# Key and query projections in neighbouring PSUM banks, numerators across two banks, and one VectorE instruction where there were two

## The chip, the core and the metric

The kernel is one program on one core of a Trainium2 chip. The metric is the time of the program on the device, in microseconds (us). The core has five engines that each work through their own queue in order: TensorE (PE, matmuls), VectorE (DVE), ScalarE (ACT), GpSimd (POOL) and SyncE (SP, which issues most DMAs). An engine waits where the next instruction of its queue is not ready. PSUM, where matmuls write, has eight banks of 512 float32 per partition.

## The reference

Random-feature attention, and then a mixture of eight experts of which each token takes the best one:

```
q_s, k_s = q * D**-0.25, k * D**-0.25
phi(x):  proj = x @ omega.T;  h = proj - sum(x*x)/2;  h -= max(h);  exp(h)/sqrt(m)
q_p, k_p = phi(q_s), phi(k_s)
kv = k_p.T @ v;  z = sum over s of k_p
out = (q_p @ kv) / (q_p @ z + 1e-6)                     # 8 batches, 8 heads, 576 x 64, 128 features
x = out, rows of 512 (4608 tokens)
e = argmax(x @ w_gate);  gate = softmax(x @ w_gate)[e];  eom = sigmoid(x @ w_output_gate)
y = gate * eom[e] * (relu(x @ w1[e]) @ w2[e])           # 8 experts, 512 -> 1024 -> 512
```

## The kernel before

**Attention** runs in 32 units `u`: a stage `j` of two batches (four stages) times a head (eight). A unit has 1152 rows in nine chunks of 128. For three groups `g` of three chunks TensorE projects keys and queries (`pp`, line 502): keys on its upper 64 rows, queries on its lower 64, each side into a bank of its own. VectorE then takes, for each side apart, the largest of 128 features of three chunks (`least`, line 524, a minimum, since the sign is turned) and turns it into the bias of the exponential (`bias`: line 530 in the first eight units, which fold the squares into the matmul, lines 533 and 537 in the others). ScalarE makes the exponentials from PSUM (`exps`, line 543, three instructions of 128 features for a side and group) and sets the bank free. The keys' exponentials and the values give `kv` (line 639), which gets eight gate columns twice through lines 677 to 700. The queries' exponentials are turned (by TensorE in the first eight units, later by a DMA transpose, line 620) and multiplied with `kv` (`attend`, line 713): a numerator `pn` of 81 columns for each of nine chunks, chunks 0 to 4 in one bank and 5 to 8 in another. `divide` (lines 722, 724, 726) makes, for each of the two banks, the divisor, its reciprocal, and the product `xf`.

**Routing.** Behind the eighth unit of a stage, `route`, `counts` (`pos`, lines 890 to 900), `ranks`, `places`, `table`, `assign` and `lists`, a chain of some fifty small VectorE instructions, sort the stage's tokens by expert. TensorE makes the list of tokens (`pid`, line 1146), VectorE turns it into indices (`gi`, line 1178; for the last list a small matmul `again`, line 1162, comes between). 38 **items** of up to 128 tokens of one expert follow: GpSimd gathers the rows (`gx`, line 1436), a DMA turns them (`xt`, line 1448), TensorE computes `ph` (line 1473) in two halves of 48 matmuls and `po` (line 1504) in two halves of 12. Lists 0, 1 and 2 hand out 8, 8 and 9 items, and the last list the other 13. An item can start only when its list exists, its rows are gathered, and they are turned.

**What sets the order.** `Plan.order` is a list scheduler in Python. Each step names its engines, costs, predecessors and banks. The planner always emits the step that can start first by its own costs and, among steps within 0.1 us, the one of the lowest rank. Attention's ranks lie below those of the items, so the items fill the holes of attention. The emitted order is each engine's queue, and on the chip an engine never leaves it. Units up to 11 take any of eight banks; later units have five (class `a`), items three (class `b`). A bank is taken when a step starts and set free by the last step that reads it.

Of the kernel before, what the change touches and what calls it, by code (L numbers as in the profile page):

```python
# [10 lines left out]
F32 = mybir.dt.float32  # L11
# [3 lines left out]
AF = mybir.ActivationFunctionType  # L15
ALU = mybir.AluOpType
# [18 lines left out]
W = 1 + D + GW  # L35
FC = F // P
# [87 lines left out]
class Plan:  # L124
# [16 lines left out]
    def add(  # L141
        self, key, engine, cost, fn, after=(), rank=0.0, tiles=(), bank=None, frees=(), dma=0.0, turn=False, early=None, cols=None,
        lead={},
# [7 lines left out]
        s.update(frees=frees, dma=dma, turn=turn, tiles=sorted(set(tiles)), early=early, part=self.part, lead=lead)  # L151
# [29 lines left out]
    def order(self):  # L181
# [17 lines left out]
        bank_cls["e"] = range(b0)  # L199
        dma_free = 0.0  # L200
# [4 lines left out]
        while ready:  # L205
            best = None
            for k in ready:
# [3 lines left out]
                if s["bank"]:  # L211
                    free = sorted(bank_free[b] for b in bank_cls[s["bank"][0][0]] if b in bank_free)
                    t = max(t, free[len(s["bank"]) - 1] if len(free) >= len(s["bank"]) else 1e9)
# [11 lines left out]
            for cls, name, _ in s["bank"]:  # L225
                b = min((b for b in bank_cls[cls] if b in bank_free), key=lambda b: bank_free[b])
                del bank_free[b]
                self.bank_of[name] = b
# [36 lines left out]
def attention_moe(ctx: ExitStack, tc: tile.TileContext, kqt, kqn, v, om, wg, w1, w2, cf, cm, ci, out):  # L265
# [38 lines left out]

    plan = Plan({"a": 5, "b": 3})
# [15 lines left out]


# [82 lines left out]
    nb = buf("nb", 2, [NC], F32)  # L405
# [47 lines left out]
    def unit(u):  # L453
# [52 lines left out]
        for g in range(G):  # L506
            x = min(g, len(parts) - 1)
            before_ = [("lo", u, x), ("const", "omh")]
            if g or u:
# [4 lines left out]
                bank=[(cls, ("pp", 2 * u + i, g), [4, M]) for i in range(2)], cols=3072.0 if whole else 1152.0,  # L514
# [3 lines left out]
        for i, nm in enumerate(("k", "q")):  # L518
            n = 2 * u + i

            def least(g, n=n):

                pp = banks["pp", n, g]
                nc.vector.tensor_reduce(out=pp[:, 3, 0:3], in_=pp[:, 0:3, :], op=ALU.min, axis=AX.X)  # L524

            def bias(g, i=i, n=n):
                c = slice(3 * g, 3 * g + 3)
                pp = banks["pp", n, g]
                if whole:
                    nc.vector.tensor_scalar(nb(n)[:, c], pp[:, 3, 0:3], SK, LIFT, ALU.mult, ALU.add)  # L530
                    return
                sq = sqs(u)[:, i, c]
                nc.vector.scalar_tensor_tensor(
                    out=pp[:, 3, 4:7], in0=pp[:, 3, 0:3], scalar=SK, in1=sq, op0=ALU.mult, op1=ALU.add
                )
                yield
                nc.vector.scalar_tensor_tensor(  # L537
                    out=nb(n)[:, c], in0=pp[:, 3, 4:7], scalar=LIFT, in1=sq, op0=ALU.add, op1=ALU.subtract
                )

            def exps(g, n=n):
                for c in range(3 * g, 3 * g + 3):
                    nc.scalar.activation(  # L543
                        ef(n)[:, c, :], banks["pp", n, g][:, c % 3, :], AF.Exp, bias=nb(n)[:, c : c + 1], scale=-SK
                    )

            for g in range(G):
                plan.add(
                    ("mx", n, g), ("DVE",), 0.47, lambda g=g, f=least: f(g), after=[("pp", u, g)], rank=R + i,
                )  # L550
                plan.chain(
                    ("nb", n, g), ("DVE",), (0.1,) if whole else (0.1, 0.1), lambda g=g, f=bias: f(g), rank=R + i,
                    after=[("mx", n, g)] + ([] if whole else [("sqr", u)]), tiles=[("nb", n)] + ([] if whole else [("sqs", u)]),
                )
                plan.add(
                    ("ex", n, g), ("ACT",), 0.76, lambda g=g, f=exps: f(g), after=[("nb", n, g)], rank=R + i,
                    tiles=[("nb", n), ("ef", n)], frees=[("pp", n, g)],
                )
# [1090 lines left out]
```

## Time and profile before

| what | value |
|---|---|
| median of three runs | 665.9 us (665.75, 665.9 and 674.13) |
| the profiled execution | 672.7 us, of which its span is 670.9 us |
| mean granted TensorE clock in it | 0.956 |
| PE busy | 614.1 us, 92% of the span |
| DVE busy | 423.9 us, 63% |
| ACT busy | 413.4 us, 62% |
| POOL busy | 341.3 us, 51% |

"Busy" of an engine is the union of its instructions' recorded times. An instruction on VectorE can be recorded from before the one ahead of it has ended, so the sum of the recorded times is above the busy time. A wait is put down to what ended it. The granted clock (PEclk) is the share of full speed at which TensorE was let run in a stretch.

### The profile page before, as it was taken

The numbers are of one execution on the slowest core, as the hardware profiler recorded it, in microseconds if no ns is written. First come the engines' busy times: TensorE is split into PE (matmuls) and PEld (weight loads), VectorE is DVE, ScalarE is ACT, GpSimd is POOL, SyncE is SP. The second block draws the span as 40 slices with busy tenths as digits, with TensorE's granted clock in tenths as the row PEclk, the third lists the DMA queues.
The fourth block names the chain that finished last, engine by engine and source line by source line (L and its number), as shares of the span: only waits on it lengthen the run. The fifth ranks groups of instructions, "written<-read, shape, count | busy, mean of one in ns | idle before, by whom it ended". The sixth has DMA issues, their size and how long they took to land. (4 is left out here: it accounts for less than half of the span.)

```text
span 670.9 us, 22907 instructions
## 1 busy us (share of the span) xinstructions
PE 614.1 (92%) x8732; PEld 484.2 (72%) x8732; DVE 423.9 (63%) x1271; ACT 413.4 (62%) x970; POOL 341.3 (51%) x235
## 2 busy tenths in 40 slices
PE   6999975889988999999989989999999899999972
PEld 6899864767676777777767777777777677686761
DVE  4899897867749899667876976562783521431160
ACT  5876896679768877888867677863611511431150
POOL 1352455659854887879658668875131122121220
PEclk9999988689988999999997989999999899999996
DMA  9544688898899898889997675666947555732730
GB/s 315 209 130 127 184 282 206 231 210 193 232 364 239 187 239 207 218 220 271 336 212 202 148 162 151 117 138 201 240 102 222 177 86 175 232 85 66 261 110 14
DMA packets 145900, 129.15 MB, mean 192 GB/s; under 512 B 104270, under 2 KB 127440, under 8 KB 144464
## 3 DMA queue, kind: packets, MB, share of 16 engines
q1 hardware_dynamic: 139760, 107.45, 62.3%
q0 software_dynamic: 5984, 19.72, 9.0%
q8 instruction: 86, 1.41, 0.9%
q14 instruction: 70, 0.57, 0.3%
HBM read 83.86 MB, written 19.30 MB: 154 GB/s over the span
## 5 line engine op out<-in xcount | busy, mean ns | idle before, releaser
L1473 PE MATMUL ph<-xt,w1h 128*128 128x128 f16 (+1 forms) x2432 | 209.4, 220 | 2.4 <-ACT hh L1480 0.9
L1473 PE MATMUL ph<-xt,w1l 128*128 128x128 f16 (+1 forms) x1216 | 204.9, 220 | 2.0 <-DVEq L1397 1.0
L543 ACT ACTIVATE ef<-pp,nb 128x128 f32<-128x128 f32 x576 | 164.4, 391 | 46.5 <-DVE nb L537 26.7
L1473 PEld LDWEIGHTS <-w1h 128*128 128x128 f16 x2432 | 184.5, 100 | 11.4 <-issue 1.9
L1484 DVE SCALAR_TENSOR_TENSOR hl<-ph,hh 128x512 f16<-128x512 f32 (+1 forms) x76 | 50.7, 667 | 118.5 <-ACTq L1402 74.4
L566 POOL TENSOR_TENSOR es<-ef,es 128x1152 f16<-128x1152 f32 x44 | 105.2, 2392 | 37.2 <-ACT es L564 29.7
L1473 PEld LDWEIGHTS <-w1l 128*128 128x128 f16 x1216 | 120.0, 100 | 2.5 <-DVEq L1397 1.4
L524 DVE TENSOR_REDUCE pp<-pp 128x3 f32<-128x384 f32 x192 | 103.1, 557 | 23.2 <-PE pp L502 18.2
L1436 POOL DMA_INDIRECT gx<-rows,gi x38 | 39.1, 1030 | 133.1 <-ACT os L1557 100.0
L1504 PE MATMUL po<-w2h,hh 128*128 128x512 f16 x280 | 106.4, 380 | 0.0
L1504 PE MATMUL po<-w2h,hl 128*128 128x512 f16 x280 | 106.1, 379 | 0.0
L1504 PE MATMUL po<-w2l,hh 128*128 128x512 f16 x280 | 106.1, 379 | 0.0
L1504 PEld LDWEIGHTS <-hh 128*128 128x128 f16 x560 | 51.4, 98 | 54.9 <-issue 0.4
L1480 ACT ACTIVATE hh<-ph 128x512 f16<-128x512 f32 (+1 forms) x76 | 44.6, 586 | 75.0 <-PE ph L1473 62.2
L1557 ACT ACTIVATE os<-po,gx 128x512 f32<-128x512 f32 (+1 forms) x38 | 25.5, 670 | 69.5 <-PE po L1504 62.2
L436 POOL TENSOR_TENSOR xlo<-xt,xhi 128x1152 f16<-128x1152 f32 x24 | 57.1, 2381 | 19.8 <-ACT xhi L429 19.4
L564 ACT CAST es<-ef 128x1152 f16<-128x1152 f32 x44 | 50.8, 1165 | 11.0 <-DMA et<-es 8.0
L713 PE MATMUL pn<-kvs,et 128*128 128x81 f16 (+1 forms) x960 | 48.0, 209 | 9.0 <-DMA et<-es 3.2
L713 PEld LDWEIGHTS <-et 128*128 128x128 f16 (+1 forms) x960 | 41.0, 105 | 16.1 <-issue 4.5
L1504 PEld LDWEIGHTS <-hl 128*128 128x128 f16 x280 | 27.4, 98 | 33.1 <-issue 0.2
L747 POOL TENSOR_TENSOR xs<-xf,xs 128x576 f16<-128x576 f32 x32 | 42.0, 1312 | 17.4 <-DVE xs L743 16.3
L502 PE MATMUL pp<-omh,xhi 64*128 64x128 f16 x432 | 43.3, 224 | 4.1 <-ACT ef L543 2.8
(181 smaller groups left out, 1059.8 us busy)
## 6 DMA issues: line engine op xcount, KB each, us to landing
r<-w SPq DMA_DIRECT2D x10, 2048.0 KB, 8.8
xt<-kqt SPq DMA_DIRECT2D x32, 576.0 KB, 5.3
xn<-kqn SPq DMA_DIRECT2D x24, 576.0 KB, 5.5
rawv<-v SPq DMA_DIRECT2D x32, 325.0 KB, 4.2
rows<-xs SPq DMA_DIRECT2D x16, 576.0 KB, 4.9
r<-w SPq DMA_DIRECT2D x8, 512.0 KB, 7.1
ef<-w SPq DMA_DIRECT2D x2, 512.0 KB, 3.9
et<-w SPq DMA_DIRECT2D x2, 512.0 KB
```

The lines of the kernel that those rows point to most:

```text
L436: lambda t0=t0, t1=t1: nc.gpsimd.tensor_tensor(out=xl(u)[:, t0:t1], in0=xt32(u)[:, t0:t1], in1=xh(u)[:, t0:t1], op=ALU.subtract),
L502: nc.tensor.matmul(banks["pp", 2 * u + i, g][:, c, :], x[r, t], w[r, :], start=(a == 0), stop=(a == len(ops) - 1))
L524: nc.vector.tensor_reduce(out=pp[:, 3, 0:3], in_=pp[:, 0:3, :], op=ALU.min, axis=AX.X)
L543: nc.scalar.activation(ef(n)[:, c, :], banks["pp", n, g][:, c % 3, :], AF.Exp, bias=nb(n)[:, c : c + 1], scale=-SK)
L564: nc.scalar.copy(es(slot_es(n))[:, 0], ef(n))
L566: nc.gpsimd.tensor_tensor(out=es(slot_es(n))[:, 1], in0=ef(n), in1=es(slot_es(n))[:, 0], op=ALU.subtract)
L713: nc.tensor.matmul(pn[lo:hi, c - c0, :], a[:, c, lo:hi], w[:, b, :], start=(i == 0), stop=(i == len(ops) - 1))
L747: nc.gpsimd.tensor_tensor(out=x[:, :, P + o : P + o + D], in0=xf(u)[:, :, 0:D], in1=x[:, :, o : o + D], op=ALU.subtract)
L1473: nc.tensor.matmul(ph[:, f4, 0:w_], w[qd][:, kk, fo : fo + P], xt(n)[:, x, 0:w_], start=(a == 0), stop=(a == 3 * KC - 1))
L1480: nc.scalar.activation(hh(n)[:, sl, 0:w_], banks["ph", n, g][:, :, 0:w_], AF.Relu)
L1484: nc.vector.scalar_tensor_tensor(out=hl(n)[:, sl, 0:w_], in0=banks["ph", n, g][:, :, 0:w_], scalar=0.0, in1=hh(n)[:, sl, 0:w_], op0=ALU.ma ...
L1504: nc.tensor.matmul(po, x(n)[:, f, :], w[f // 2][:, f % 2, :], start=(f == 0 and a == 0), stop=(f == FC - 1 and a == 2))
```

## The change

Three things, and what they need in the planner:

- PSUM is one tile of eight banks, and a step's banks are views of it. A step can ask for banks that lie beside each other (`beside`). The planner waits for a pair of free neighbours and, among pairs that are free, takes the one with the fewest free banks next to it.
- Keys' and queries' projections of a group lie in neighbouring banks. `least` and `bias` take both sides in one instruction, 2 x 3 results, and the bias tile `nb` holds both sides of a unit. `exps` stays three instructions for each side and now waits for the bias of both.
- The numerators of all nine chunks lie in two neighbouring banks at a step of 105 columns, so that no chunk crosses from one bank into the next. `attend` writes all nine and `divide` takes all nine at once: three instructions where there were six.

```
-                bank=[(cls, ("pp", 2 * u + i, g), [4, M]) for i in range(2)], ...
+                bank=[(cls, ("pp", 2 * u + i, g), [4, M]) for i in range(2)], beside=True, ...
...
-                pp = banks["pp", n, g]
-                nc.vector.tensor_reduce(out=pp[:, 3, 0:3], in_=pp[:, 0:3, :], op=ALU.min, axis=AX.X)
+            pp = both_sides(g)
+            nc.vector.tensor_reduce(out=pp[:, :, 3, 0:3], in_=pp[:, :, 0:3, :], op=ALU.min, axis=AX.X)
...
+        for g in range(G):
+            plan.add(("mx", u, g), ("DVE",), 0.9, lambda g=g: least(g), after=[("pp", u, g)], rank=R)
+            plan.chain(("nb", u, g), ("DVE",), (0.1,) if whole else (0.1, 0.1), lambda g=g: bias(g), ...)
...
-                    ("mx", n, g), ("DVE",), 0.47, lambda g=g, f=least: f(g), after=[("pp", u, g)], rank=R + i,
...
-                    ("ex", n, g), ("ACT",), 0.76, lambda g=g, f=exps: f(g), after=[("nb", n, g)], rank=R + i,
+                    ("ex", n, g), ("ACT",), 0.76, lambda i=i, g=g: exps(i, g), after=[("nb", u, g)], rank=R + i,
...
-        for c0, c1, pe, dve in ((0, 5, 0.6, 0.48), (5, NC, 0.42, 0.4)):
-                ("pn", u, c0), ("PE",), pe, lambda c0=c0, c1=c1: attend(c0, c1), ..., bank=(cls, ("pn", u, c0), [c1 - c0, W]),
-                ("xf", u, c0), ("DVE",), (0.07, 0.1, dve), lambda c0=c0, c1=c1: divide(c0, c1), ...
+            ("pn", u), ("PE",), 1.02, attend, ..., bank=[(cls, ("pn", u, i), [512]) for i in range(2)], beside=True,
+            ("xf", u), ("DVE",), (0.08, 0.1, 0.85), divide, ...
...
+        def places(s):
+            cls, n = bank_cls[s["bank"][0][0]], len(s["bank"])
+            if s["beside"]:
+                return [tuple(range(b, b + n)) for b in cls if b + n - 1 in cls]
+            return list(itertools.combinations(cls, n))
+        def pick(s, t):
+            ...
+            return min(places(s), key=lambda bs: (late(bs), alone(bs), bs))
...
-                    t = max(t, free[len(s["bank"]) - 1] if len(free) >= len(s["bank"]) else 1e9)
+                    t = max(t, min(max(bank_free.get(b, 1e9) for b in at_) for at_ in places(s)))
...
-                banks[name] = ps.tile([P, *shape], F32, tag=f"bank{b}", name="_".join(str(x) for x in name))
+                banks[name] = shaped(psum[:, plan.bank_of[name], 0 : math.prod(shape)], shape)
```

The other costs, ranks, shifts and the counts of items stay. Since the planner works with other costs and other places for banks, it emits another order on all engines. Three places:

VectorE, groups 1 and 2 of one unit (`pp_1` and `pp_2`; the higher number of a name is the queries' side) before:

```order
L524 TENSOR_REDUCE pp_2_5601<-pp_2_5601 128x3
L533 SCALAR_TENSOR_TENSOR pp_1_5573<-pp_1_5573,sqs_4157 128x3
L533 SCALAR_TENSOR_TENSOR pp_2_5601<-pp_2_5601,sqs_4157 128x3
L537 SCALAR_TENSOR_TENSOR nb_5392<-pp_1_5573,sqs_4157 128x3
L537 SCALAR_TENSOR_TENSOR nb_5392<-pp_2_5601,sqs_4157 128x3
L524 TENSOR_REDUCE pp_1_5574<-pp_1_5574 128x3
```

And VectorE at one group of a unit after the change, where lines 555, 564 and 568 are the old 524, 533 and 537, and `psum` stands for every bank:

```order
L555 TENSOR_REDUCE psum<-psum 128x2x3
L776 CAST xs_6350<-xf_6976 128x9x64
L1409 UNCONDITIONAL_BRANCH
L564 SCALAR_TENSOR_TENSOR psum<-psum,sqs_5520 128x2x3
L568 SCALAR_TENSOR_TENSOR nb_6658<-psum,sqs_5520 128x2x3
L478 TENSOR_REDUCE sqs_7028<-sqt_6654 128x9x2
```

One chain of three per group is left where two ran side by side, and inside it each step reads what the one ahead of it in the chain wrote.

TensorE behind the list of tokens of stage 1 (`pid`) before, the first row of each step (`ph_0_5497` and `ph_1_5626` belong to the eighth item, `ph_0_5994` to the ninth, the first that needs this list):

```order
L1146 MATMUL pid_5399<-r_itc,place 128x16
...
L713 MATMUL pn_0_5428<-kvs_5046,et_5182 128x81
...
L1473 MATMUL ph_0_5497<-xt_4752,w1h_90 128x128
...
L502 MATMUL pp_1_5573<-omh,xhi_4608 128x128
...
L1473 MATMUL ph_1_5626<-xt_4752,w1h_92 128x128
...
L1504 MATMUL po_5701<-w2h_98,hh_5593 128x512
...
L713 MATMUL pn_0_5777<-kvs_5334,et_5558 128x81
...
L1504 MATMUL po_5701<-w2h_100,hh_5593 128x512
...
L639 MATMUL kv_5909<-vs_5068,es_5775 128x65
...
L1473 MATMUL ph_0_5994<-xt_5683,w1h_90 128x128
```

And after it (lines 1179, 1537, 671, 533, 709 and 1506 are the old 1146, 1504, 639, 502, 677 and 1473):

```order
L1179 MATMUL psum<-r_itc,place 128x16
...
L1537 MATMUL psum<-w2h_101,hh_4725 128x512
...
L671 MATMUL psum<-vs_4172,es_4792 128x65
...
L533 MATMUL psum<-omh,xhi_4193 128x128
...
L709 MATMUL psum<-cmt,kvs_5160 64x128
...
L533 MATMUL psum<-omh,xhi_4678 128x128
...
L671 MATMUL psum<-vs_4494,es_5216 128x65
...
L1506 MATMUL psum<-xt_5175,w1h_91 128x128
```

Between the list and the first item that needs it stood a whole item (two halves `ph`, two halves `po`), two numerators and other attention steps; now half a `po`, two `kv` and pieces of other steps stand there, and no `ph` and no `pn`. Behind the list of stage 2 an item has moved ahead in the same way: half a `po` and a numerator are left of it there.

TensorE behind `again`, which completes the last list, before:

```order
L1162 MATMUL a_g_a_i_n<-r_once,ident 64x24
...
L1504 MATMUL po_11822<-w2h_100,hh_11680 128x512
...
L1473 MATMUL ph_0_11959<-xt_11528,w1h_90 128x128
...
L1473 MATMUL ph_1_12041<-xt_11528,w1h_92 128x128
...
L1504 MATMUL po_12107<-w2h_98,hh_12091 128x512
...
L1473 MATMUL ph_0_12185<-xt_12035,w1h_90 128x64
```

And after it:

```order
L1195 MATMUL psum<-r_once,ident 64x24
...
L1537 MATMUL psum<-w2h_99,hh_11233 128x512
...
L1537 MATMUL psum<-w2h_101,hh_11233 128x512
...
L1506 MATMUL psum<-xt_11359,w1h_91 128x64
```

One half `po`, two halves `ph` and two halves `po` stood between it and the first item of the last list; now two halves `po` do.

More of the change, by code (lines that the diff above doesn't have):

```diff
@@ L1 @@
+import itertools
 import math
@@ L35 @@
 W = 1 + D + GW
+PN = 105
+assert 4 * PN + W <= 512 <= 5 * PN and (NC - 1) * PN + W <= 1024
 FC = F // P
@@ L224, in order @@
             ready.remove(k)
[L225 to L228, printed above, removed]
+            if s["bank"]:
+                for b, (_, name, _) in zip(pick(s, t), s["bank"]):
+                    del bank_free[b]
+                    self.bank_of[name] = b
             if s["eng"] == ("PE",):
```

120 lines of the change are left out of this document (67 added, 53 removed).

## The prediction

> **What bounds the kernel now.** I read the page first: TensorE (PE) is busy 92% of the span, so a cheaper VectorE (DVE) pays only where PE waits for it. Next came busy time by stretch. The columns are the stretch, its length, then busy us of PE, PE's weight loads, DVE, ACT and POOL, the granted clock (PEclk), the DMA share and GB/s.
>
> ```profile
> 20.00:85.00 65.00, 63.65 (x883) 57.52 (x880) 57.59 (x162) 50.95 (x164) 26.80 (x19) 1.00 0.49 154
> 85.00:130.00 45.00, 32.13 (x424) 28.16 (x423) 37.94 (x161) 31.97 (x88) 24.59 (x17) 0.77 0.85 236
> 130.00:254.00 124.00, 115.39 (x1738) 89.86 (x1737) 92.30 (x289) 99.29 (x230) 90.49 (x56) 0.96 0.93 239
> 254.00:386.00 132.00, 126.11 (x1955) 97.29 (x1953) 100.12 (x317) 101.85 (x233) 96.90 (x63) 0.97 0.91 225
> 386.00:523.00 137.00, 134.98 (x1941) 102.62 (x1938) 81.13 (x260) 71.06 (x161) 72.64 (x53) 0.99 0.67 166
> ```
>
> PE idles 1.4 us in 20 to 85, 12.9 in 85 to 130, 8.6 in 130 to 254, 5.9 in 254 to 386 and 2.0 in 386 to 523. Behind 523 only items are left, which the change does not touch. DVE is the busiest engine in one stretch alone, 85 to 130, where it is at 84%, PE at 71% and the clock at 0.77. There, ahead of the first list, no item can fill PE's holes. The waits (total, times, longest) name the chain:
>
> ```profile
> ACT ef L543 <- DVE nb L537: 26.7, 20, 3.5
> ...
> PE pp L502 <- ACT ef L543: 3.4, 6, 0.9
> ```
>
> ScalarE waits 26.7 us for the bias, but PE waits for a bank only six times, 3.4 us in all.
>
> **The change part by part.** First, the joined instructions on VectorE. In the groups by line, the numbers behind the bar are total busy us and mean ns of one.
>
> ```profile
> L524 DVE TENSOR_REDUCE pp<-pp 128x3 f32<-128x384 f32 x192 | 103.1, 557 | 23.2 <-PE pp L502 18.2 <-ACT kvf L688 3.7 <-ACT kvs L695 0.6
> ...
> L447 DVE TENSOR_REDUCE sqs<-sqt 128x18 f32<-128x1152 f32 x24 | 32.3, 1347 | 0.9 <-ACT sqt L442 0.5
> ...
> L533 DVE SCALAR_TENSOR_TENSOR pp<-pp,sqs 128x3 f32<-128x3 f32 x144 | 22.5, 162 | 0.6 <-DVEq L1397 0.2
> L537 DVE SCALAR_TENSOR_TENSOR nb<-pp,sqs 128x3 f32<-128x3 f32 x144 | 21.6, 156 | 3.0 <-ACT ef L543 0.3
> L726 DVE TENSOR_TENSOR xf<-pn,den 128x400 f32<-128x400 f32 x32 | 18.3, 572 | 1.0
> L726 DVE TENSOR_TENSOR xf<-pn,den 128x320 f32<-128x320 f32 x32 | 15.5, 486 | 0.4
> ...
> L530 DVE TENSOR_SCALAR nb<-pp 128x3 f32<-128x3 f32 x48 | 6.7, 151 | 0.1
> ...
> L722 DVE TENSOR_SCALAR den<-pn 128x5 f32<-128x5 f32 x32 | 5.1, 159 | 33.3 <-PE pn L713 33.1 <-PE kv L677 0.2
> ```
>
> A reduction of 768 elements is not in the trace. Between 384 and 1152 elements the reductions grow by (1347 − 557) / 768 = 1.03 ns an element, so one of 768 takes 557 + 384 × 1.03 = 952 ns and replaces 1114: 162 ns less, 96 times, 15.6 us. Lines 533 and 537 lose 72 instructions each, of 162 and 156 ns: 22.9 us. Line 530 loses 24 of 151: 3.6 us. For a numerator one product of 720 elements takes 572 + 320 × (572 − 486) / 80 = 916 instead of 1058 ns, and a divisor of 159 ns goes, and a reciprocal, which I put at the divisor's price, less some 0.02 us for the longer ones that stay: 0.14 + 0.16 + 0.16 − 0.02 = 0.44 us, 32 times: 14 us. In recorded time 56 us go, 1.75 us per unit.
>
> Recorded time is not time taken. The timeline of VectorE (start, length, what):
>
> ```profile
> 86.44 1.01 DVE L524 TENSOR_REDUCE pp<-pp 128x3 f32<-128x384 f32 x2
> 87.36 0.15 DVE L533 SCALAR_TENSOR_TENSOR pp<-pp,sqs 128x3 f32<-128x3 f32 x1
> 87.62 0.16 DVE L537 SCALAR_TENSOR_TENSOR nb<-pp,sqs 128x3 f32<-128x3 f32 x1
> ```
>
> Two reductions of 557 ns stand in 1.01 us, so the second began 0.10 us before the first had ended. About that overlap is already enjoyed by each of the 360 instructions that go (96 + 144 + 24 + 96), so 56 − 36 = 20 us are really set free, 0.6 us per unit; with no overlap it is 1.75. The opposite shows too: lines 533 and 537, which depend on each other, start 0.26 us apart, and before the second side's instruction could stand in that hole. The joined chain has nothing of its own for it. I take 1.1 us per unit, about half of the way; bounds 0.6 and 1.75. How many units pass through a stretch shows in the reductions of line 524 in it, six a unit:
>
> ```profile
> 20.00:85.00 65.00, 20.49 (x38) 1.00 0.49 154
> 85.00:130.00 45.00, 11.79 (x22) 0.77 0.85 236
> ```
>
> In 85 to 130 these are 22 / 6 = 3.7 units, and the relief is 3.7 × 1.1 = **−4** (bounds −2 and −6.5). In 20 to 85 PE runs 98% of the time and hides it: nothing, and if that cover failed the 38 / 6 = 6.3 units would bring −7. From 130 on PE has items and attention to run, and its idle time there is made of transfers and lists: **−1** (bounds 0 and −14.5, all idle time of 130 to 386). ScalarE's exponentials of the keys now wait for the queries' bias, 0.95 instead of some 0.56 us behind the projection. With banks free (six waits in all), that is latency only: nothing; its price without that cover is a rival below.
>
> Second, what moved. The order has fewer and shorter pieces between each list and the first item that needs it. The pace of such pieces, from the chain that ended last:
>
> ```profile
> 446.89 0.93 PE kv L639 x30
> 447.82 2.59 PE po L1504 x12
> 450.41 0.23 PE kv L677 x4
> 450.64 0.61 PE pp L502 x18
> 451.25 0.34 PE kv L682 x2
> 451.59 2.59 PE po L1504 x12
> 454.18 2.68 PE ph L1473 x48
> 456.86 1.24 PE pn L713 x30
> ```
>
> How long list, gather and transpose take shows in the start and length of the list's matmuls and in the start of the first transpose that needs it (`pid` stages 1 and 2, `again`):
>
> ```profile
> 254.08 0.60 PE L1146 MATMUL pid<-r_itc,place 128*128 128x16 f16 x18
> ...
> 385.32 0.83 PE L1146 MATMUL pid<-r_itc,place 128*128 128x18 f16 x27
> ...
> 509.68 0.29 PE L1162 MATMUL a_g_a_i_n<-r_once,ident 128*64 128x24 f32 x2
> ```
>
> ```profile
> 263.08 1.24 SPq L1448 DMA_TRANSPOSE xt<-gx  x1
> ...
> 395.50 1.24 SPq L1448 DMA_TRANSPOSE xt<-gx  x1
> ...
> 515.50 1.31 SPq L1448 DMA_TRANSPOSE xt<-gx  x1
> ```
>
> And the DMA issues, whose last number is us from issue to landing:
>
> ```profile
> gx<-rows,gi POOLq DMA_INDIRECT x38, 4.3
> xt<-gx SPq DMA_TRANSPOSE x38, 3.4
> ```
>
> From list to turned rows: 263.08 + 3.4 − 254.68 = 11.8 us; 395.50 + 3.4 − 386.15 = 12.75; 515.50 + 3.4 − 509.97 = 8.9. What stands on PE meanwhile:
>
> - Stage 1: before, two `ph`, two `po`, two `pn`, three `pp` and smaller pieces, 16.4 us, which covers 11.8. After: `po`, two halves of `kv`, twice, three `pp`, and 0.57 us of gate columns: 2.59 + 2 × 0.93 + 3 × 0.61 + 0.57 = 6.85. PE stands 5.0 us.
> - Stage 2: before 17.9, which covers 12.75. After: `po`, `pn`, one pair of `kv` halves, four `pp` and 0.80 of gate columns: 8.0. PE stands 4.75 us.
> - The last list: before three halves `po` and two `ph`, 13.1, which covers 8.9. After two `po`, 5.2. PE stands 3.7 us.
>
> That is 13.5 us. With the bare transfers (4.3 + 3.4, and some 0.7 us to the first gather, an estimate from the 0.26 us between dependent instructions) the chain is 8.4 us, the three waits are 1.6, 0.4 and 3.2, and the sum 5.2: the lower bound. The items have not vanished: what stood here runs earlier, where PE now and then idles. Of the 14.5 us that PE idles in 130 to 386, I let the moved item fill a third of the 13.5: **+9** (bounds 2 and 13.5).
>
> Third, the clock. Behind a stall PE runs slower:
>
> ```profile
> 353.35 0.64 PE L682 MATMUL kv<-wgr,kvf 128*128 128x32 f32 x2 [2.92 <-ACT kvf L688]
> ```
>
> ```profile
> 350.00:360.00 10.00, 6.93 (x88) 6.36 (x86) 3.78 (x11) 8.22 (x22) 6.28 (x5) 0.66 0.89 180
> ```
>
> Around a wait of 2.92 us the clock's mean over 10 us was 0.66, so 3.4 us of full speed were withheld, and of these some 1.5 (3.07 idle at half) cost nothing. About 1.9 us for each of three stalls, two thirds of which stand: **+4** (bounds 0 and 6). The Trainium skill, page "TensorE: Matmul & The Clock Gate", section "Part 1: The HAM clock gate (the "warmup" mystery)", says that after idling the array runs at half rate for about 3.4 us before full rate is granted. By it each stall costs 1.7 us, and the term would be 5 with all three; the trace's 1.9 agrees in size.
>
> Sum: −4 − 1 + 9 + 4 = **+8** on the profiled execution's 672.7 us: 680.7. The median is 665.9, 6.8 below it; on that basis 674.
>
> **The rivals.**
>
> *Nothing shows.* The DVE chain gives 4 us, the lists take 4, since the gathers of the new order start sooner. For it: the lower bound of the stalls, 5.2. Against it: POOL and SP have other work queued between. 666.
>
> *Every recorded nanosecond comes back.* If instructions on VectorE did not overlap, 85 to 130 gains 6.5 us, half of PE's idle time there, and the sooner bias halves the rest of 85 to 386 too (12.9 + 8.6 + 5.9 = 27.4): −13.7, with the lists' stalls swallowed by what PE gains ahead of them. For it: ACT's 26.7 us of waiting for the bias. Against it: the two reductions in 1.01 us, and PE's six waits for ACT. 652. The Trainium skill, page "VectorE: DVE Perf Modes", section "The DRAIN you can't avoid", says that a VectorE instruction starts only once the pipe has emptied behind the one before; by that rule each one that goes would take its fixed cost with it, and the relief in the forecast's sum would be 6.5, not 4. The trace's 0.10 us of overlap speaks against the strict form.
>
> *Neighbours are late* (the side of slower). From the twelfth unit on attention has five banks, in which a pair must lie side by side. The keys' bank, free first, must then idle until the queries' three exponentials have read theirs.
>
> ```profile
> L543 ACT ACTIVATE ef<-pp,nb 128x128 f32<-128x128 f32 x576 | 164.4, 391 | 46.5 <-DVE nb L537 26.7
> ```
>
> Three take 3 × 164.4 / 576 = 0.86 us. PE's queue is in order, so the items behind a waiting `pp` wait too. Of 60 groups half would cost 26 us, less 5 of relief: +21, 687. It decides from about 21 groups: (13.3 + 5) / 0.86. For it: the planner, whose own costs set the pairs, knows no such latency. Against it: a projection took two banks before as well.
>
> **How the numbers follow.** Two per cent, 13.3 us, is about what a measurement of this kernel can tell from no change: under 652.6 is faster, over 679.2 slower. The forecast has 0.42, with a range of its own from 668 to 681, and a tenth of it is over 679.2. Nothing shows: 0.10. Every nanosecond: 0.25, of which 0.15 is under 652.6, since the halved idle time stands just at that bound. Late neighbours: 0.23, all over. So faster 0.15, same 0.58, slower 0.27. The range 652 to 688 leaves out about half of the third case's lower part and a part of the last beyond 688, together 0.2.
>
> **What would show it.** Relief: DVE's busy time falls by 20 to 56 us from 423.9, and 85 to 130 gets shorter by about 4. Lists: PE stands 3 to 5 us ahead of the first `ph` of items 8, 16 and 25, with PEclk low behind each. Late neighbours: "PE pp waits for ACT ef" rises from 3.4 us to over 15. It is wrong if PE does not stand at the lists, or if its idle time between 130 and 386 falls by more than 5 us without any stall of that kind.

## The result, and the profile after

The changed kernel takes 691.4 us (median of four runs, 687.85 to 696.67), the kernel before 666.43 us beside it: 1.035 times, with a 95% interval of 1.025 to 1.046. It is slower by some 24 us, where 8 were forecast, and beyond the range's end of 688. Ratios here and below leave out executions over 1.5% longer than the fastest of their kernel, while the medians include them. The profiled execution took 690.92 us, with a span of 688.9.

First the windows by stretch, laid around each list in both kernels so that the same part of the program stands in the same row (columns as in the prediction: stretch, length, busy us of PE, weight loads, DVE, ACT, POOL, granted clock, DMA share, GB/s). Before:

```profile
90.00:152.00 62.00, 47.57 (x632) 40.13 (x633) 47.00 (x196) 45.65 (x126) 33.99 (x22) 0.81 0.88 219
152.00:242.00 90.00, 83.47 (x1295) 65.14 (x1292) 67.20 (x192) 72.27 (x163) 66.27 (x43) 0.96 0.92 246
242.00:284.00 42.00, 40.69 (x668) 31.56 (x666) 34.84 (x129) 32.80 (x78) 34.30 (x23) 1.00 0.91 218
284.00:374.00 90.00, 85.80 (x1311) 66.31 (x1306) 65.89 (x192) 71.52 (x160) 65.93 (x43) 0.96 0.94 241
374.00:426.00 52.00, 49.64 (x787) 38.93 (x784) 36.91 (x141) 37.12 (x92) 39.05 (x25) 0.97 0.59 137
...
500.00:535.00 35.00, 32.42 (x457) 24.72 (x455) 16.33 (x37) 12.24 (x17) 6.03 (x6) 0.95 0.64 192
```

And the changed kernel:

```profile
90.00:152.00 62.00, 46.09 (x583) 37.82 (x583) 46.46 (x132) 43.44 (x115) 33.64 (x21) 0.81 1.01 249
152.00:242.00 90.00, 87.04 (x1356) 66.99 (x1350) 62.38 (x130) 70.09 (x159) 61.84 (x40) 1.00 0.92 226
242.00:284.00 42.00, 33.74 (x522) 27.39 (x517) 28.93 (x84) 26.68 (x65) 27.74 (x18) 0.84 0.75 188
284.00:382.00 98.00, 95.19 (x1475) 72.20 (x1473) 67.31 (x141) 79.62 (x179) 73.80 (x46) 1.00 0.89 234
382.00:434.00 52.00, 43.47 (x694) 34.95 (x692) 34.77 (x95) 32.90 (x81) 37.91 (x25) 0.90 0.65 159
...
521.00:556.00 35.00, 26.93 (x362) 21.36 (x361) 17.49 (x37) 11.69 (x15) 5.68 (x6) 0.86 0.65 184
```

Around the lists of stages 1 and 2 and the last list (rows three, five and six) PE stands 1.3, 2.4 and 2.6 us before, and 8.3, 8.5 and 8.1 us after, at a clock of 0.84 to 0.90. Between the lists (rows two and four) it is the other way: PE stands less than before, and the clock is full.

The same windows, with the rest of the span, give a full account of one execution of each kernel. "Idle" is a window's length less PE's busy time. "Low" is half of the time in which PE was busy while the clock's records grant 0.50. Span less both is 593.2 us before and 592.8 after, so the losses are all that differs, to within half a us.

| part of the program | before: idle + low | after: idle + low | difference |
|---|---|---|---|
| the first 90 us | 7.5 + 0.0 | 7.6 + 0.0 | +0.1 |
| first list | 14.4 + 9.4 | 15.9 + 10.1 | +2.2 |
| between first and second | 6.5 + 3.3 | 3.0 + 0.0 | -6.8 |
| list of stage 1 | 1.3 + 0.0 | 8.3 + 4.8 | +11.8 |
| between | 4.2 + 3.2 | 2.8 + 0.0 | -4.6 |
| list of stage 2 | 2.4 + 1.7 | 8.5 + 4.5 | +9.0 |
| between | 0.0 + 0.0 | 0.3 + 1.4 | +1.7 |
| last list | 2.6 + 1.7 | 8.1 + 3.8 | +7.6 |
| items alone | 17.8 + 1.7 | 16.9 + 0.2 | -2.5 |
| sum | 77.7 | 96.1 | +18.5 |

The difference of the spans is 18.0 us. What PE waits for at the three lists shows in the timeline of PE (start, length, matmuls; in brackets the wait and what ended it):

```profile
260.06 1.81 PE L671 MATMUL psum<-vs,es 128*128 128x65 f16 x30 [3.28 <-issue]
264.25 0.64 PE L714 MATMUL psum<-wgr,kvf 128*128 128x32 f32 x2 [0.95 <-ACT kvf L720]
...
269.75 1.72 PE L671 MATMUL psum<-vs,es 128*128 128x65 f16 x28 [1.55 <-POOL es L598]
...
402.83 0.43 PE L748 MATMUL psum<-kvs,et 128*128 128x81 f16 x4 [3.60 <-ACT ef L575]
406.70 0.29 PE L533 MATMUL psum<-omh,xhi 64*128 64x128 f16 x2 [1.61 <-DVE xf L761]
...
539.90 0.27 PE L1506 MATMUL psum<-xt,w1h 128*128 128x64 f16 x2 [3.22 <-DMA xt<-gx]
```

Only at the last list does PE wait for the turned rows of the first item. At the other two it stands ahead of steps of attention (`kv`, gate columns, a numerator, a projection). The first of these waits, 3.28 us, is a load of PE's own (the last section has it). The numerator and the projection at the list of stage 2 wait last for a bank that another step has still to read out (lines 575 and 761). The others wait for another engine's step of the same unit. Without an item between them attention runs by its own chain, and at a low clock, as three windows behind the list of stage 1 show:

```profile
257.00:260.00 3.00, 0.00 (x0) 0.00 (x0) 0.51 (x3) 0.76 (x3) 1.17 (x2) 0.89 1.13 172
260.00:263.00 3.00, 2.94 (x52) 2.62 (x51) 1.00 (x5) 1.58 (x5) 1.42 (x2) 0.50 0.78 211
...
266.00:269.00 3.00, 2.20 (x37) 1.84 (x36) 1.88 (x4) 3.00 (x5) 2.15 (x2) 0.50 1.13 175
```

The VectorE groups (total busy us, mean ns of one behind the bar):

```profile
L555 DVE TENSOR_REDUCE psum<-psum 128x6 f32<-128x768 f32 x96 | 90.8, 960 | 28.7 <-PE psum L533 28.3
...
L776 DVE CAST xs<-xf 128x576 f16<-128x576 f32 x32 | 36.0, 1126 | 0.4
...
L761 DVE TENSOR_TENSOR xf<-psum,den 128x720 f32<-128x720 f32 x32 | 29.0, 906 | 2.6
...
L564 DVE SCALAR_TENSOR_TENSOR psum<-psum,sqs 128x6 f32<-128x6 f32 x72 | 11.8, 165 | 0.5
L568 DVE SCALAR_TENSOR_TENSOR nb<-psum,sqs 128x6 f32<-128x6 f32 x72 | 11.6, 162 | 1.7
```

The joined reduction takes 960 ns and the joined product 906, where 952 and 916 were reckoned. But DVE's busy time falls only from 423.9 to 413.6 us. And the waits (total, times, longest):

```profile
ACT ef L575 <- DVE nb L568: 34.0, 23, 4.1
...
PE psum L533 <- DVE xf L761: 3.9, 4, 1.6
...
PE psum L533 <- ACT ef L575: 2.1, 1, 2.1
```

ScalarE waits longer for the bias than before (26.7 us), and projections wait once, not six times, for exponentials to read out a bank. But they also wait 3.9 us for products to read out theirs (line 761), where this was 0.6 us before.

### The profile page after: what moved, and what is told of

Its sections match the earlier page's. It is cut to its first block, busy times and chain, and to the rows that moved or that the text cites. A ratio compares the mean times of both kernels' runs of the same rounds, so it can differ in the third digit from the quotient of the medians.

```text
span 688.9 us, 22514 instructions
## 1 busy us (share of the span) xinstructions
PE 617.6 (90%) x8732; PEld 485.8 (71%) x8732; DVE 413.6 (60%) x911; ACT 413.5 (60%) x970; POOL 342.5 (50%) x235
## 5 line engine op out<-in xcount | busy, mean ns | idle before, releaser
L1506 PE MATMUL psum<-xt,w1h 128*128 128x128 f16 (+1 forms) x2432 | 209.9, 220 | 7.4 <-issue 3.2
L1506 PE MATMUL psum<-xt,w1l 128*128 128x128 f16 (+1 forms) x1216 | 205.5, 220 | 2.2 <-DVE w1l L399 1.9
L575 ACT ACTIVATE ef<-psum,nb 128x128 f32<-128x128 f32 x576 | 163.0, 401 | 55.3 <-DVE nb L568 34.0
L1506 PEld LDWEIGHTS <-w1h 128*128 128x128 f16 x2432 | 185.3, 100 | 15.4 <-issue 8.5
L1517 DVE SCALAR_TENSOR_TENSOR hl<-psum,hh 128x512 f16<-128x512 f32 (+1 forms) x76 | 50.6, 666 | 126.7 <-ACTq L1435 69.5
L598 POOL TENSOR_TENSOR es<-ef,es 128x1152 f16<-128x1152 f32 x44 | 104.8, 2396 | 22.9 <-ACT es L596 22.8
L1537 PE MATMUL psum<-w2h,hh 128*128 128x512 f16 x280 | 107.0, 382 | 1.5 <-DVE hl L1517 1.2
L555 DVE TENSOR_REDUCE psum<-psum 128x6 f32<-128x768 f32 x96 | 90.8, 960 | 28.7 <-PE psum L533 28.3
L1537 PE MATMUL psum<-w2h,hl 128*128 128x512 f16 x280 | 106.6, 381 | 1.2 <-DVE hl L1517 1.2
L1537 PE MATMUL psum<-w2l,hh 128*128 128x512 f16 x280 | 106.6, 381 | 0.0
L1513 ACT ACTIVATE hh<-psum 128x512 f16<-128x512 f32 (+1 forms) x76 | 44.5, 585 | 80.5 <-PE psum L1506 73.7
L748 PE MATMUL psum<-kvs,et 128*128 128x81 f16 (+1 forms) x960 | 48.4, 209 | 11.3 <-DVE kvs L732 5.3
```

What stands on the lines that cost most here:

```text
L555: nc.vector.tensor_reduce(out=pp[:, :, 3, 0:3], in_=pp[:, :, 0:3, :], op=ALU.min, axis=AX.X)
L575: nc.scalar.activation(ef(n)[:, c, :], banks["pp", n, g][:, c % 3, :], AF.Exp, bias=nb(u)[:, i, c : c + 1], scale=-SK)
L598: nc.gpsimd.tensor_tensor(out=es(slot_es(n))[:, 1], in0=ef(n), in1=es(slot_es(n))[:, 0], op=ALU.subtract)
L748: nc.tensor.matmul(pn[lo:hi, c, :], a[:, c, lo:hi], w[:, b, :], start=(i == 0), stop=(i == len(ops) - 1))
L1506: nc.tensor.matmul(ph[:, f4, 0:w_], w[qd][:, kk, fo : fo + P], xt(n)[:, x, 0:w_], start=(a == 0), stop=(a == 3 * KC - 1))
L1513: nc.scalar.activation(hh(n)[:, sl, 0:w_], banks["ph", n, g][:, :, 0:w_], AF.Relu)
```

## The experiments

The ratio in each is to the kernel before, run beside it on the same chip, with its 95% interval. "Cover" names the us of TensorE work that an order has between each of the three later lists and the first item of that list, by the paces of the prediction: 16.9 (16.4 in the prediction), 17.9 and 13.1 in the kernel before, 6.8, 8.0 and 5.2 in the changed one.

**Instructions against order.** The changed kernel's order and banks, with each joined instruction split:

```diff
-            nc.vector.tensor_reduce(out=pp[:, :, 3, 0:3], in_=pp[:, :, 0:3, :], op=ALU.min, axis=AX.X)
+            for i in range(2):
+                nc.vector.tensor_reduce(out=pp[:, i, 3, 0:3], in_=pp[:, i, 0:3, :], op=ALU.min, axis=AX.X)
...
```

The steps of the bias and of the division are split in the same way.

> The changed kernel with its order, banks and places kept to the letter, but each joined VectorE instruction split again into two (a side each, or chunks 0 to 4 and 5 to 8). Theory L (the lists: the new order leaves too little for TensorE behind each list of tokens, and the joined instructions themselves help by about 5 us): 5 us over the changed kernel's 691.4, so 696, between 692 and 701, with PE standing behind the three lists as before. Rival J (the joined instructions are what costs, since keys' exponentials wait for the queries' bias): 8 to 24 us under it, 667 to 683.

Measured: 699.35 us, 1.047 (1.041 to 1.053). Theory L's range holds it. Split instructions are not faster: rival J is out. Against the changed kernel's 1.035 (1.025 to 1.046) the joining is worth some 1%, but the intervals overlap. The new order with its banks, and VectorE's instructions as small as in the kernel before, costs 4.7%.

**An item held behind each list.**

```diff
+    HOLD = {7: ("pid", 1), 15: ("pid", 2), 24: ("again", 3)}
...
                 after=[("xt", n), *cuts_of(n, 1, halves_of[g])]
+                + ([HOLD[n]] if g == 0 and n in HOLD else [])
```

> The changed kernel with one rule more for the planner: the last item of a list (items 7, 15 and 24) may not start before the matmuls of the next list. Behind the three lists now stand 15.4, 16.0 and 10.5 us of TensorE work (6.8, 8.0 and 5.2 in the changed kernel, 16.9, 17.9 and 13.1 in the kernel before). Theory L: the waits behind the lists and the low clock after them go, 15 to 20 of the 23 us that they cost, so 672 to 677. Rival P (late neighbours: pairs of banks make projections wait): nothing of that goes away, 686 to 693. Rival R (the engines' loads of registers from memory, 3.2 us on PE behind the list of stage 1, 3.1 on ACT and DVE at that of stage 2, stand there whatever is queued): 683 to 688.

Measured: 688.58 us, 1.030 (1.023 to 1.038). Cover was back to 15.4, 16.0 and 10.5 us, and almost nothing was won: theory L, my reading of the stalls until then, fell. By the ratio it would be some 687 us beside 666.4, in the ranges of rivals P and R. Rival R's loads were short in this run, though, at most 1.3 us at the list of stage 1 and 1.9 at that of stage 2, so long loads are not what the time is lost by. Its windows around the three lists:

```profile
246.00:288.00 42.00, 36.82 (x542) 28.58 (x541) 29.46 (x90) 27.12 (x66) 27.83 (x18) 0.88 0.76 182
385.00:437.00 52.00, 46.53 (x738) 37.79 (x738) 35.99 (x104) 37.23 (x94) 39.14 (x26) 0.90 0.73 164
519.00:554.00 35.00, 26.20 (x364) 19.33 (x362) 18.58 (x42) 11.45 (x15) 4.92 (x5) 0.96 0.61 179
```

PE still stands 5.2, 5.5 and 8.8 us there, but now partly ahead of the list, in two views of its timeline:

```profile
255.04 0.29 PE L533 MATMUL psum<-omh,xhi 64*128 64x128 f16 x2 [1.60 <-DVE xf L761]
256.98 0.65 PE L1179 MATMUL psum<-r_itc,place 128*128 128x16 f16 x18 [0.80 <-DVE r_itc L1063]
...
529.15 0.29 PE L1195 MATMUL psum<-r_once,ident 128*64 128x24 f32 x2 [3.20 <-DVE r_once L1190]
```

The list's own matmuls wait for VectorE (lines 1179 and 1195). An item kept for the time behind a list is missing ahead of it. I read this so: the lists come late for the items, and where the last item of the old list stands only moves the hole. From here on this is theory A: attention gets on more slowly than the items beside it. Late means beside the items and not in absolute time: the list of stage 1 starts at 253.58 us in the changed kernel and at 254.08 before.

**Each part alone.** The numerators joined and the projections as in the kernel before:

```diff
-                bank=[(cls, ("pp", 2 * u + i, g), [4, M]) for i in range(2)], beside=True, cols=...
+                bank=[(cls, ("pp", 2 * u + i, g), [4, M]) for i in range(2)], cols=...
...
-            plan.add(("mx", u, g), ("DVE",), 0.9, lambda g=g: least(g), after=[("pp", u, g)], rank=R)
+                    ("mx", n, g), ("DVE",), 0.47, lambda g=g, f=least: f(g), after=[("pp", u, g)], rank=R + i,
```

> One part of the change alone: numerators of nine chunks in two neighbouring banks with joined divisors; the projections, their reductions and biases as before, in any two banks. The order has 27.1, 11.2 and 10.5 us of TensorE work behind the three lists. Theory L: only the second list is short, by 1 to 2 us; the joined divisors bring 1 to 2 us: 664 to 670. Rival P (pairs of banks): numerators must wait for two neighbours, 675 to 685.

Measured: 681.21 us, 1.019 (1.012 to 1.026), in rival P's range and out of theory L's. And the reverse, the projections joined and the numerators in two steps:

```diff
-            ("pn", u), ("PE",), 1.02, attend, ..., bank=[(cls, ("pn", u, i), [512]) for i in range(2)], beside=True,
+        for c0, c1, pe, dve in ((0, 5, 0.6, 0.48), (5, NC, 0.42, 0.4)):
+                ("pn", u, c0), ("PE",), pe, lambda c0=c0, c1=c1: attend(c0, c1), ..., bank=(cls, ("pn", u, c0), [c1 - c0, W]),
```

> The other part alone: projections in neighbouring banks and joined reductions and biases; numerators in two steps as before. The order has 7.7, 7.1 and 2.6 us of TensorE work behind the three lists. Theory L: the same stalls as in the changed kernel, a little longer at the last list: 688 to 696. Rival N (the numerators' pair, taken at once, is what costs): 664 to 672.

Measured: 692.97 us, 1.037 (1.031 to 1.044). The projections' part makes as much of a loss as the whole change; theory L's range holds this one, and rival N is out. The numerators' part also loses, which theory L did not expect with a cover of 27.1, 11.2 and 10.5 us.

**Parts of the planner.** The kernel before, with one rule of the changed planner (and its banks as views of one tile), then with a second:

```diff
-                b = min((b for b in bank_cls[cls] if b in bank_free), key=lambda b: bank_free[b])
...
+            return min(places(s), key=lambda bs: (late(bs), alone(bs), bs))
```

> The kernel before with only the changed planner's way of choosing free banks (one tile of eight banks, any two of them for a projection); no pairs, no joined instruction. The order has 11.8, 14.8 and 7.9 us of TensorE work behind the three lists, where the kernel before has 16.9, 17.9 and 13.1. Theory A (attention's projections get their banks later, item halves of 2.6 us go ahead of them, so items run out before the lists are there): little of that here, 0 to 6 us over the kernel before, 667 to 673. Rival T (any other order than the one that was there costs this much): 680 to 692.

Measured: 684.72 us, 1.021 (1.013 to 1.029). By the ratio this is 14 us. Theory A, which gave it 6 at most, missed; rival T's range begins here. The way of choosing among free banks costs more than the forecast gave the whole change, with no pair and no joined instruction in the kernel.

```diff
-                bank=[(cls, ("pp", 2 * u + i, g), [4, M]) for i in range(2)], ...
+                bank=[(cls, ("pp", 2 * u + i, g), [4, M]) for i in range(2)], beside=True, ...
```

> The same, and the two banks of a projection must be neighbours; instructions and their dependencies are those of the kernel before. 10.9, 10.8 and 2.6 us of TensorE work behind the three lists. Theory A: 8 to 16 us over the kernel before, 675 to 683, since a projection now also waits for two free neighbours. Rival K (only that keys wait for the queries' side counts): as the run with the new choice of banks alone, within 3 us.

Measured: 1.044 times (1.033 to 1.056), some 696 us beside 666.4; rival K is out. The demand for neighbours costs a further 2%, and with it the loss is no smaller than that of the whole changed kernel. It is nearly 30 us where theory A gave 16 at most.

```diff
-                    ("ex", n, g), ("ACT",), 0.76, ..., after=[("nb", n, g)], rank=R + i,
+                    ("ex", n, g), ("ACT",), 0.76, ..., after=[("nb", 2 * u + x, g) for x in range(2)], rank=R + i,
```

> The run with the new choice of banks alone, and one dependency more in the planner: keys' exponentials stand behind both sides' biases, as they must in the changed kernel; any two banks, separate instructions. 16.3, 9.4 and 5.2 us of TensorE work behind the three lists. Theory A: 7 to 15 us over the kernel before, 674 to 682. Rival B (only the pairs of banks count): within 3 us of the run with the new choice alone.

Measured: 682.35 us, 1.016 (1.008 to 1.025), no more than with the choice of banks alone. Both ranges hold it: by the ratio it is 11 us over the kernel before, where theory A said 7 to 15, and it lies within 3 us of the run with the choice of banks alone. But that choice alone already cost 14 us. Keys that wait for the queries' bias cost nothing on top that can be seen, so this leg of theory A is not borne out.

**The same instructions, another order.** The changed kernel with a planner that takes the joined reduction for short:

```diff
-            plan.add(("mx", u, g), ("DVE",), 0.9, lambda g=g: least(g), after=[("pp", u, g)], rank=R)
+            plan.add(("mx", u, g), ("DVE",), 0.47, lambda g=g: least(g), after=[("pp", u, g)], rank=R)
```

> The changed kernel, instructions and banks by its rules, but its planner is told 0.47 us for the joined reduction (0.9 in the changed kernel; the chip takes 0.96). So the order puts attention's next steps ahead of items although they are ready only later: 27.5, 19.5 and 5.2 us of TensorE work stand behind the three lists. Theory A with the order as its carrier: attention keeps its lead over the items, 12 to 19 us under the changed kernel's 691.4, so 672 to 679. Rival C (the length of the joined chain on the chip is what costs, whatever the order): 686 to 694.

Measured: 685.88 us, 1.023 (1.014 to 1.031); beside it the kernel before took 672.37 us, so the ratio counts, and it would be some 682 us beside 666.4. It lies between the two ranges. Some third of the loss went with an order alone, less than theory A asked for, and the interval overlaps that of the changed kernel.

**One tile of PSUM.** The new choice of banks replaced by "the one that came free first", which gives the order of the kernel before, step for step; what is left of the change is that banks are views of one tile.

```diff
-            return min(places(s), key=lambda bs: (late(bs), alone(bs), bs))
+            return min(places(s), key=lambda bs: (late(bs), max(bank_free.get(b, 1e9) for b in bs), ...))
```

> The kernel before, step for step in its own order and in its own banks, but with the banks as views of one PSUM tile, as in the changed kernel. Theory O (the order is what the new choice of banks costs): as the kernel before, within 4 us. Rival V (views of one tile bring waits of another kind): 10 to 16 us over it, like the run with the new choice of banks alone.

Measured: 667.09 us, 1.0015 (0.998 to 1.005). Rival V is out: views cost nothing. What the new choice of banks cost in the run above is its order, or which banks the steps got in it; the two change together in every run here.

**Other orders of the kernel before.** One number of the planner's ranks each:

```diff
-SHIFT = {..., 'mx': 0.5, 'nb': -0.4, 'ex': -2.0, ...}
+SHIFT = {..., 'mx': 0.5, 'nb': -0.4, 'ex': -2.5, ...}
```

> The kernel before with one number of its planner moved: the exponentials' rank by -0.5. Instructions, tiles, banks and rules stay; 242 of 569 TensorE steps stand elsewhere, and 18.9, 13.0 and 10.5 us of TensorE work stand behind the three lists. Theory U (the order there was is a lucky one among its like, and nearly any other costs some 10 us): 672 to 682. Rival A (only late attention costs, and here nothing makes it late): 664 to 670.

Measured: 671.4 us, 1.006 (1.001 to 1.011), between the two ranges.

```diff
-SHIFT = {..., 'mx': 0.5, 'nb': -0.4, 'ex': -2.0, ...}
+SHIFT = {..., 'mx': 1.0, 'nb': -0.4, 'ex': -2.0, ...}
```

> A second one of this kind: the reductions' rank by +0.5 in the kernel before; 275 of 569 TensorE steps stand elsewhere, and 22.9, 23.8 and 13.1 us of TensorE work stand behind the three lists, more than in the kernel before. Theory U: 672 to 682. Rival A: 664 to 670.

Measured: 682.65 us, 1.022 (1.013 to 1.031), though it has the most cover of all behind its lists. So the kernel before, with its own instructions and rules, loses half a per cent in one case and two in the other when one rank moves. Theory U holds for the second.

**New ranks for the changed kernel.** All ranks replaced by others that the planner's own reckoning prefers; instructions, pairs and rules are the changed kernel's.

```diff
-SHIFT = {'hi': -1.4, 'lo': 0.3, 'sqa': 1.9, 'sqr': 2.3, 'T': 1.8, 'pp': 0.1, 'mx': 0.5, ...}
+SHIFT = {'hi': -5.0, 'lo': 4.2, 'sqa': 1.5, 'sqr': -2.6, 'T': -1.9, 'pp': -7.4, 'mx': -0.7, ...}
```

> The changed kernel with other ranks for its planner, searched for by the planner's own reckoning with its new instructions; 14.8, 13.0 and 10.5 us of TensorE work stand behind the three lists (6.8, 8.0 and 5.2 in the changed kernel). Theory A or U: most of the loss goes, 668 to 678, as the joined instructions themselves bring 8. Rival C (the joined chain's length on the chip costs whatever the order): 684 to 692.

Measured: 673.63 us, 1.011 (1.007 to 1.015). Two thirds of the loss go with nothing but ranks; theory A or U's range holds it, and rival C is out. The windows around its three lists:

```profile
235.00:277.00 42.00, 40.99 (x608) 29.92 (x602) 32.08 (x96) 27.62 (x68) 27.50 (x18) 1.00 0.72 170
371.00:423.00 52.00, 48.33 (x775) 37.01 (x773) 38.80 (x106) 37.83 (x96) 36.84 (x26) 1.00 0.71 164
502.00:537.00 35.00, 31.15 (x432) 24.37 (x430) 18.63 (x39) 12.50 (x17) 8.04 (x8) 0.90 0.71 203
```

PE stands 1.0, 3.7 and 3.9 us, close to the kernel before, and the clock is full at the first two. The same order with split instructions, by the first experiment's edit:

> The changed kernel with the new ranks of the last run, its order and banks kept to the letter, but each joined VectorE instruction split in two again. Theory D (joined instructions are worth some 1.1% wherever VectorE's chain of small steps stands ahead of a list): 1.6 to 2.6% over the kernel before (the run with the new ranks: 1.1%). Rival E (they are worth something only in an order in which TensorE has nothing else to do): 0.7 to 1.4% over it.

Measured: 678.04 us, 1.014 (1.009 to 1.018) where joined instructions gave 1.011 (1.007 to 1.015). In this order joining is worth 0.3%, which can't be told from nothing. The result is at the upper end of rival E's range and below theory D's, though its interval reaches into that.

**The numerators' part with ranks of its own, and the kernel before searched in the same way.** The edits are the numerators' part alone, other ranks, and the choice of banks of the run with one tile; in the second run only other ranks.

```diff
-SHIFT = {'hi': -1.4, 'lo': 0.3, 'sqa': 1.9, ..., 'T': 1.8, 'pp': 0.1, ...}
+SHIFT = {'hi': 10.4, 'lo': 21.2, 'sqa': -11.0, ..., 'T': -58.7, 'pp': -3.0, ...}
```

> The numerators' part alone, with ranks searched for it, and where banks are equally good those that came free first. 20.6, 18.5 and 10.5 us of TensorE work stand behind the three lists. Theory A (what costs is that projections get banks and biases later, and these stay as they were): 0 to 2% under the kernel before, 655 to 667. Rival U (no other order of this kind reaches the one that was there): 0.5 to 2% over it.

Measured: 666.48 us beside 670.26 of the kernel before, 0.994 (0.991 to 0.998). Theory A's range holds it. This is the one version that beats both kernels, the kernel before by 0.6%.

```diff
-SHIFT = {'hi': -1.4, 'lo': 0.3, 'sqa': 1.9, 'sqr': 2.3, 'T': 1.8, ...}
+SHIFT = {'hi': 0.6, 'lo': 0.3, 'sqa': 5.4, 'sqr': 4.7, 'T': 2.8, ...}
```

> The kernel before with ranks from the same search by the planner's own reckoning; nothing else changes. 16.3, 13.0 and 10.5 us of TensorE work stand behind the three lists. Theory A: within 1% of the kernel before. Rival U: 0.5 to 2% over it.

Measured: 678.06 us, 1.011 (1.008 to 1.015). Rival U's range holds it and theory A's, by a little, does not. The order that the kernel before came with is better than the one that the same search finds for it. With ranks from that search both kernels stand at 1.011, the one before and the changed one. So where both got their orders in the same way, one order each, no difference can be seen. The other 2.4% the changed kernel loses under the ranks that it took over.

## Why the prediction was right and wrong

- **What bounds the kernel**: right. All of the difference is time in which PE had nothing to do or ran at a low clock; the work at full speed is the same 593 us.
- **Relief of VectorE** (-5 in the sum): durations were right within 2%, but the gain is not where I put it. In 85 to 130 DVE's busy time rose. The first list starts 1.1 us sooner (117.23 us before, 116.09 after), but its losses did not fall; they rose by 2.2 us where I had -4:

```profile
85.00:130.00 45.00, 33.76 (x460) 30.02 (x460) 39.18 (x121) 33.80 (x92) 24.44 (x16) 0.77 0.98 255
```

  DVE's total fell by 10.3 us, below my lower bound of 20. Part of that is the cast of line 743 (now 776), whose shape is unchanged: 32 of 1126 ns, before 871, so 8.2 us came back there. With the order held, joining lowered DVE's busy time by 16.4 us (430.0 split, 413.6 joined) and, with the new ranks, by 18.1 (418.7 and 400.6): some 0.5 us per unit, half of the 1.1 that I took. Splitting cost 1.1% in one order and 0.3% in the other, 8 and 2 us, neither clear of noise. A term of 5 us is within that.
- **Stalls at the lists** (+9): this step failed. The places were right, all three, and so was the time from list to turned rows: 11.0 and 10.7 us at stages 1 and 2, where I had 11.8 and 12.75. What failed is the cover. I took the pieces behind a list as solid work, which PE goes through at its pace and then stands once, for the rows of the first item. This is what happened at the last list (3.22 us, forecast 3.7). At the other two the pieces, 6.85 and 8.0 us by my reckoning, took 17.1 and 16.5 us from the list's end to the first `ph`, since each waited for a load, for attention's own steps or for a bank, and went at half clock between the waits. The rows were there some 6 us before PE was. At the three lists PE's idle time grew by 18.6 us (24.9 less 6.3), where the sum has 13.5 before what the moved items fill.
- **The clock behind them** (+4): mis-sized, since I read the trace wrongly. I took the 3.07 us without a matmul in 350 to 360 to lie in the slow stretch. Most of them lie ahead of it: in 350 to 353 PE was busy for 0.43 us at a clock of 1.00, in 353 to 360 for 6.50 us at 0.51. So that stall withheld 3.2 us, not 1.9. Two others in the kernel before withheld 1.7 each (the lists of stage 2 and the last one in the table). The three lists lost 9.8 us more by the clock than before (13.1 less 3.4), with a stretch at 0.50 from 260 to 273 us. The Trainium skill, page "TensorE: Matmul & The Clock Gate", section "Part 1: The HAM clock gate (the "warmup" mystery)", gives about 3.4 us at half rate, by an estimate 1.7 us a stall. The trace has this behind two single waits, but the lists of stages 1 and 2 lost 4.8 and 4.5 us, since waits followed each other.
- **What the moved items fill**: I let it take a third off the stalls, 4.5 us. Between the lists PE gained 11.4 us (6.8 and 4.6). So lists and clock cost 28.4 less 11.4, 17.0 us, where the sum has 13.
- **The deeper error**: I took the holes for a matter of what stands behind a list. The held items show that cover alone is not it: with 15.4, 16.0 and 10.5 us back, 3.0% was still lost, and the order with 22.9, 23.8 and 13.1 lost 2.2%. That the lists are late for the items, and cover a sign of that and not its cause, is my reading; theory A, which says so, missed its range in four runs.
- **Rival "neighbours are late"**: its 687 us came nearest, and neighbours do cost (1.021 to 1.044 in the planner's parts). But its mechanism was seen only in small. It was to show as projections that wait on the chip for exponentials, over 15 us; these waits fell from 3.4 to 2.1 us. Waits for products to read out a pair came on top, 3.9 us for 0.6. The planner sees a missing pair when it makes the order and can put an item ahead, so most of the price should lie in the order; no run shows this by itself.
- **Rival "every nanosecond comes back"**: out. DVE's busy time fell by 10.3 us and not by 56, and splitting cost some 8 us in one order and 2 in the other. The section of the Trainium skill that this rival names goes on to say that an instruction which is not held starts earlier; the 0.10 us of overlap agree with that.
- **The range** ended at 688 because the forecast's two terms had bounds of their own of 13.5 and 6; their sum with no relief at all, 19.5, would have made 685, so no choice inside those bounds reaches 691. Another 6.8 us of the miss come from the way from the profile to the median: I took them off because the profiled execution of the kernel before was that much above its median, but that of the changed kernel, at 690.9, is no higher than its own. On the profiled executions the change is 18.2 us where the sum has 8; lists and clock make 4 us of that miss, and most of the rest is relief that the table does not show.

What stays open: which property makes an order good, and whether it is the sequence of the steps or the banks that come with it. Cover of 25 us and less in all three places together (the changed kernel, its split, the projections' part, the neighbours alone) went with losses of 3.5% and over; but orders with 31 us and more lie anywhere between 0.994 and 1.030.

## What to carry to other kernels

Where a planner makes the order, a change of costs, banks or rules is two changes, the instructions and a new order, and here the second cost some 31 us, and the first gained 2 to 8, which is not clear of noise. Time them apart: keep the order and split the instructions, and move one rank of the old kernel to see how wide its orders lie (here 0.6 and 2.2%). Then give the new version ranks of its own before it is judged; the part that lost 1.9% as it came gained 0.6% with ranks and a choice of banks of its own.

## What was not expected of the hardware

Engines load control words of a new list from memory into registers (`TENSOR_LOAD` from `ctl` in the trace), and the first loads of a list take longer than the others of the kind. At the list of stage 1 in the changed kernel the trace has, by engine's sequencer (start, length in us):

```
256.42 2.14 POOL   256.83 3.21 PE   257.75 2.78 DVE   257.87 2.65 ACT   258.85 1.86 SP
```

Four of the five end between 260.0 and 260.7, and during them PE does nothing (0.00 of the 3 us from 257, above); the 3.28 us that the timeline of PE puts down to "issue" are this load. In the kernel before the same loads at that list took 1.07 to 1.54 us, and PE was busy all through. At the list of stage 2 ScalarE and VectorE were held in the same way, for 3.12 and 3.18 us from 393.1 us (1.75 and 1.85 before), and neither was busy from 394 to 396. The run with held items, with short loads, lost nearly as much, so they are not the main cause. Most other loads take 0.3 to 0.8 us. What makes these long was not tried.

The cast of 576 elements a partition (line 743), with the same operands, took 810 ns on average with the new ranks, 847 in the run with one tile, 871 in the kernel before, 1074 in its first other order and 1126 in the changed kernel. Besides their orders, some of these kernels differ in joined instructions or in the one tile of PSUM; what slows the cast was not tried.
